# Sinks ahead of the values on 128 rows, and the low parts of x and g last in their groups

## The chip, the cores and the metric

The kernel runs on one core of a Trainium2 chip. The metric is the time of one execution on the device in microseconds; a kernel's time is the median of its runs. The profile comes from one execution, recorded by the hardware profiler. Its engines are PE (matrix products and transposes; PEld is its weight load, which can overlap the product before it), DVE (vector), ACT (scalar functions and copies), POOL and SP (which issues the DMAs).

## The reference

Attention with a window of 128 tokens and 4 sink tokens that every query may see, on q, k, v of shape (4 batches, 8 heads, 768 tokens, 64), then a feed-forward network of 512 to 2048 to 512 on the 3072 rows that come out:

```python
scores = scale * np.matmul(q, k.transpose(0, 1, 3, 2))
keep = is_sink | in_window
scores = np.where(keep, scores, -1000000000.0)
...
a = a / (np.sum(a, axis=-1, keepdims=True) + 1e-09)
x = np.matmul(a, v)            # then (B, S, H*D)
h = x @ w_in
sp = np.maximum(h, 0.0) + np.log1p(np.exp(-np.abs(h)))
g = h * erf(sp)
out = g @ w_out
```

## The kernel before, in words

**Tiling.** The tokens are cut into 12 groups g of 256 (three to a batch), and the 8 heads into 4 pairs c. A pair of heads in a group is one attention step, s = 4g + c, 48 in all. The network works on a group's 512 x 256 slice of x: 16 hidden blocks f of 128 features each, numbered m = 16g + f, of which two share one tile (h_0, h_2, ... h_190 name the pairs).

**An attention step.** `prep` transposes k and q (four products into tqk, L218) and copies them into kq on ACT. `score` makes the scores ps on quarters of the array (sixteen products of 64 x 64, L277); DVE masks them, ACT takes the exponential into pst (L298, four), `norm` divides. `ptrans` transposes the window's part (four products into tp, L322, copied to pt by ACT, L324, and cut to uo by POOL, L328) and the sinks' part (two products into ts, L342, copied to sp by ACT, L346). `av` multiplies with the values (L364) and `avs` with the sinks' values sv (L371), both into one tile av; `xfin` takes it into x.

**Precision.** x, w and g are split into a high and a low part. A hidden block is a sum over four slices c of (high w, high x), (high w, low x) and (low w, high x): twelve products of 128 x 256 on L544, and 24 to a pair. `act` turns a pair into g: on ACT r (L556 to L558) and three u (L561), on DVE three products with acc (L563), of which the first reads h and gives its tile back, then the high part of g on DVE (L568) and the low part on POOL (L569). `project` adds three products (L584 to L586) for each of the group's two output tiles o_0 and o_1. The first group g = 0 is computed in full precision (L540, L581) while the weights are split.

The sinks' part is three rows of 32 for each half i of the group (high, low, high of the 32 probabilities of two heads), 96 rows in all, against sv, whose rows 0 to 31, 32 to 63 and 64 to 95 hold high, high and low of the sinks' values. sv's rows 96 to 127 are zero. At the first group of a batch each step loads its sinks' values anew: POOL clears a corner of the tile v (L198), two DMAs fill it (L200), ACT copies it twice (L226), DVE makes the low part (L227).

**What sets the order.** Each engine works its own list in order. The lists come from a scheduler that simulates the program; each operation carries a priority from the slot a = m + 16 that it belongs to and from its kind (the table O: hidden 0, projections 900, scores and values -300, and so on). `core(s)` issues av of step s - 2, then the scores of s, then avs of s - 2; `follow` ties the first two together in this order. Only among the rest, mainly h and o, does the scheduler choose.

**Tiles that come round.** h has two pairs of banks: h_k and h_(k-4) use the same (pairs are numbered by twos), so h_k's first product waits for the first L563 of h_(k-4). tqk, tp, ts and av go round two banks, so av_s takes the bank of a tp, which is free once ACT has copied pt (L324). tile v has three buffers.

Of the kernel before, what the change touches and what calls it, by code (L numbers as in the profile page):

```python
# [19 lines left out]
P = 128  # L20
# [30 lines left out]
def kernel(  # L51
# [20 lines left out]
    NG = B * GPB  # L72
    NU = 4
    NSTEP = NG * NPAIR
    KB, S3 = P + SW, 6 * SW
    scale = 1.0 / math.sqrt(D)

    cpool = ctx.enter_context(tc.tile_pool(name="const", bufs=1))
# [50 lines left out]
    def fast_path():  # L129
        with ExitStack() as st:  # L130
# [43 lines left out]

            pst = pers.tile([P, RING, 2, 2, KB], F32, name="pst")

            shs = [pers.tile([P, 2, 3, 2 * SW], F32R, name=f"sh{i}") for i in range(2)]
            xp = {}

            stp = {}  # L180
# [48 lines left out]
            def core(s):  # L229

                prev = None
                late = s - AL >= NE
                if late:
                    prev = av(s - AL)
                if s < NSTEP:
                    score(s, prev)
                if late:
                    avs(s - AL)

            def av1(s):  # L240

                av(s)
                avs(s)

            def score(s, prev):

# [67 lines left out]
            def ptrans(s):  # L314
# [15 lines left out]
                        compare_op=op, fill=0.0, base=0, channel_multiplier=sg,  # L330
                    )

                sh = shs[s % 2]
                x = pst[:, s % RING, :, :, P:]
                for r in (0, 2):
                    nc.vector.tensor_copy(sh[:, :, r].rearrange("p i (h t) -> p i h t", h=2), x)
# [2 lines left out]
                    sh[:, :, 0].rearrange("p i (h t) -> p i h t", h=2).bitcast(F32), op=ALU.subtract,  # L339
                )  # L340
                for i in range(2):
                    nc.tensor.transpose(  # L342
                        out=ts[:S3, i, :], in_=sh[:, i].rearrange("p r t -> p (r t)").bitcast(F32), identity=ident
                    )
                sp = d["sp"] = work.tile([P, 2, P], F32R, tag="sp", bufs=AL, name=f"sp_{s}")
                nc.scalar.copy(sp[:S3], ts[:S3])  # L346

            def av(s):

                g, c = divmod(s, NPAIR)  # L350
                gb = g % GPB
                d = stp[s]
                vt = d["v"]
                uo = d["uo"].rearrange("p h i e t -> p h (i e t)")
                a = d["av"] = ps_t.tile([P, GT], F32, tag="t", name=f"av_{s}")
                ops = [(vt[:, 2], uo[:, :, 3 * P :], P), (vt[:, 1], uo[:, :, P : 3 * P], 0)]
                if gb > 0:
                    ops.append((vt[:, 0], uo[:, :, :P], 0))
                prev = None
                for m, (x, y, t0) in enumerate(ops):  # L360
                    for h in range(2):
                        o = a[64 * h : 64 * h + 64, t0 : t0 + y.shape[-1]]
                        prev = follow(
                            prev, nc.tensor.matmul(o, x[:, h, :], y[:, h, :], start=(m == 0), stop=False, skip_group_check=True)  # L364
                        )
                return prev

            def avs(s):

                g, c = divmod(s, NPAIR)  # L370
                nc.tensor.matmul(  # L371
                    stp[s]["av"], sv[:S3, c, :], stp[s]["sp"][:S3].rearrange("p i t -> p (i t)"),
                    start=False, stop=True, skip_group_check=True,
                )

            def xfin(s):

# [18 lines left out]
            def pos(s):  # L396

                return 3 * s if s < NE else 4 * s - 4 * NE + 3 * NE - 2

            plan = {}  # L400
            for s in range(NSTEP + AL):
                if s < NSTEP:
                    for what, fn, a in (
                        ("prep", prep, pos(s) - 3), ("norm", norm, pos(s) + 1), ("ptrans", ptrans, pos(s) + 2),
                        ("load", load, pos(s) - 4),
                    ):
                        plan.setdefault(max(a, 0 if what == "prep" else -1), []).append((what, fn, s))
                plan.setdefault(pos(s), []).append(("core", core, s))
                if s < NE:
                    plan.setdefault(pos(s) + 3, []).append(("av", av1, s))  # L410
                    plan.setdefault(pos(s) + 4, []).append(("xfin", xfin, s))
                elif s - AL >= NE:
                    plan.setdefault(pos(s) + 1, []).append(("xfin", xfin, s - AL))
# [113 lines left out]
    class make_mlp:  # L527
# [7 lines left out]
        def hidden(self, hp, xt, f):  # L535
            j, fs = f // 4, slice(f % 4 * P, f % 4 * P + P)
            o = hp[:, f % 2, :]
            if len(xt) == 1:
                for c in range(NC):
                    nc.tensor.matmul(o, wf[NC * j + c][:, fs], xt[0][:, c, :], start=(c == 0), stop=(c == NC - 1))  # L540
                return
            ops = [(c, *e) for c in range(NC) for e in ((0, 0), (0, 1), (1, 0))]
            for m, (c, p, e) in enumerate(ops):
                nc.tensor.matmul(  # L544
                    o, wt[NC * j + c][:, p, fs], xt[e][:, c, :], start=(m == 0), stop=(m == len(ops) - 1)
# [26 lines left out]
        def project(self, gt, g, f):  # L572
            if f == 0:
                for i in range(2):
                    self.acc[g, i] = self.ps_o.tile([P, DM], F32, tag="o", name=f"o_{g}_{i}")
            for i in range(2):
                o = self.acc[g, i]
                n0 = (f % 2) * GT + i * P
                ws = slice(n0, n0 + P)
                if len(gt) == 1:  # L580
                    nc.tensor.matmul(o, gt[0][:, ws], wf[16 + f], start=(f == 0), stop=(f == NF - 1))  # L581
                    continue
                gh, gl = gt
                nc.tensor.matmul(o, gh[:, ws], wt[16 + f][:, 0, :], start=(f == 0), stop=False)  # L584
                nc.tensor.matmul(o, gh[:, ws], wt[16 + f][:, 1, :], start=False, stop=False)  # L585
                nc.tensor.matmul(o, gl[:, ws], wt[16 + f][:, 0, :], start=False, stop=(f == NF - 1))  # L586

        def result(self, g, i):
            ot = self.work.tile([P, DM], F32, tag="u", bufs=UB, name=f"ot_{g}_{i}")
# [149 lines left out]
```

## Time and profile before

| | before |
|---|---|
| median of three runs | 780.71 us (778.91, 783.86, 780.71) |
| profiled execution: span | 779.7 us |
| PE busy | 728.2 us, 93% of the span |
| ACT busy | 531.3 us, 68% |
| DVE busy | 508.6 us, 65% |
| POOL busy | 204.6 us, 26% |
| from 100 us to the end: PE busy | 661.86 of 679.70 us |

The page gives the profiled execution's span and no separate time for it; the median of the runs is 1.0 us above that span. Busy time counts an engine's instructions and leaves out its waits. A row of a timeline gives the start, the length, the engine and the line, and in brackets how long the engine had been idle before and what released it. Starts on PE are more telling than lengths: products overlap, so the distance between two starts is what a product costs.

### The profile page before, as it was taken

The numbers are of one execution on the slowest core, as the hardware profiler recorded it, in microseconds if no ns is written. First come the engines' busy times: TensorE is split into PE (matmuls) and PEld (weight loads), VectorE is DVE, ScalarE is ACT, GpSimd is POOL, SyncE is SP. The second block draws the span as 40 slices with busy tenths as digits, with TensorE's granted clock in tenths as the row PEclk, the third lists the DMA queues.
The fourth block names the chain that finished last, engine by engine and source line by source line (L and its number), as shares of the span: only waits on it lengthen the run. The fifth ranks groups of instructions, "written<-read, shape, count | busy, mean of one in ns | idle before, by whom it ended". The sixth has DMA issues, their size and how long they took to land.

```text
span 779.7 us, 14925 instructions
## 1 busy us (share of the span) xinstructions
PE 728.2 (93%) x5168; PEld 605.0 (78%) x5168; DVE 508.6 (65%) x1509; ACT 531.3 (68%) x1261; POOL 204.6 (26%) x210
## 2 busy tenths in 40 slices
PE   2578998999999999999999999999999999999997
PEld 1356665788878888888888888888878888888896
DVE  6968999787465576576566476476466476475352
ACT  2245478897687577578688578488578578487474
POOL 1311121133222223232232232232222232232121
PEclk8569899999999999999999999999999999999999
DMA  6765631201211221111121121121121121010000
GB/s 196 241 196 177 228 82 29 70 22 27 70 33 28 59 51 25 48 48 27 32 72 28 41 70 25 34 63 25 31 74 28 28 75 32 11 40 1 27 2 32
DMA packets 100595, 47.33 MB, mean 61 GB/s; under 512 B 89248, under 2 KB 93344, under 8 KB 100512
## 3 DMA queue, kind: packets, MB, share of 16 engines
q1 hardware_dynamic: 100224, 46.29, 21.6%
q8 instruction: 43, 0.70, 0.4%
q14 instruction: 40, 0.33, 0.1%
q10 hardware_dynamic: 288, 0.00, 0.0%
HBM read 37.88 MB, written 6.29 MB: 57 GB/s over the span
## 4 chain that ended last, share of the span: by engine, by line
PE 79%; DVE 9%; ACT 6%; DMA 2%; issue 1%; SPq 1%; POOL 1%; ACTq 0%; DVEq 0%; POOLq 0%
PE h L544 29%; PE o L586 10%; PE o L584 10%; PE o L585 10%; PE av L364 5%; PE ps L277 5%; PE tqk L218 2%; PE tp L322 2%; PE h L540 2%; PE av L371 2%; DVE wt L473 1%; DVE gf L563 1%; ACT pst L298 1%; PE ts L342 1%; DVE w L453 1%
## 5 line engine op out<-in xcount | busy, mean ns | idle before, releaser
L544 PE MATMUL h<-xh,wt 128*128 128x256 f32 x1408 | 271.2, 283 | 5.3 <-DVE acc L563 4.1
L544 PEld LDWEIGHTS h<-xh,wt 128*128 128x128 f32 x1408 | 223.7, 189 | 11.3 <-DVE acc L563 5.6
L544 PE MATMUL h<-xl,wt 128*128 128x256 f32 x704 | 198.7, 283 | 0.0
L569 POOL TENSOR_TENSOR g<-acc,g 128x512 fp32r<-128x512 f32 x88 | 114.9, 1306 | 308.2 <-DVE g L568 211.8
L561 ACT ACTIVATE u<-r 128x512 f32<-128x512 f32 x288 | 163.5, 624 | 10.3 <-DVE wf L459 4.3
L328 POOL TENSOR_SCALAR_AFFINE_SELECT uo<-pt 128x512 f32<-128x512 f32 (+1 forms) x96 | 85.2, 909 | 250.1 <-ACT pt L324 250.1
L584 PE MATMUL o<-wt,g 128*128 128x512 f32 x352 | 141.4, 402 | 0.7 <-DVE g L568 0.7
L585 PE MATMUL o<-wt,g 128*128 128x512 f32 x352 | 139.7, 397 | 0.0
L563 DVE SCALAR_TENSOR_TENSOR acc<-u,h 128x512 f32<-128x512 f32 x88 | 60.4, 687 | 120.8 <-ACT u L561 61.2
L563 DVE SCALAR_TENSOR_TENSOR acc<-u,acc 128x512 f32<-128x512 f32 x176 | 124.7, 709 | 19.9 <-ACT u L561 6.2
L586 PE MATMUL o<-wt,g 128*128 128x512 f32 x352 | 135.3, 401 | 0.3 <-POOL g L569 0.2
L544 PEld LDWEIGHTS h<-xl,wt 128*128 128x128 f32 x704 | 132.9, 189 | 2.3
L298 ACT ACTIVATE pst<-pst,neg 128x144 f32<-128x144 f32 x192 | 77.6, 407 | 39.1 <-DVE neg L294 39.0
L556 ACT ACTIVATE r<-h 128x512 f32<-128x512 f32 x96 | 57.0, 594 | 44.0 <-PE h L544 42.6
L584 PEld LDWEIGHTS o<-wt,g 128*128 128x128 f32 x352 | 66.2, 188 | 13.4 <-ACT r L557 0.9
L586 PEld LDWEIGHTS o<-wt,g 128*128 128x128 f32 x352 | 64.8, 188 | 14.8 <-POOL g L569 1.2
L585 PEld LDWEIGHTS o<-wt,g 128*128 128x128 f32 x352 | 66.1, 188 | 12.1
L289 DVE COPY_PREDICATED ps<-tri,ps 64x256 f32<-64x256 int8 (+1 forms) x100 | 41.8, 420 | 40.3 <-PE ps L277 37.6
L558 ACT ACTIVATE r<-r 128x512 f32<-128x512 f32 x96 | 60.8, 634 | 2.5
L557 ACT ACTIVATE r<-r 128x512 f32<-128x512 f32 x96 | 60.7, 632 | 1.8
L364 PE MATMUL av<-uo,v 128*64 128x128 f32 (+1 forms) x512 | 50.1, 328 | 8.6 <-ACT pt L324 4.4
L388 ACT CAST xh<-av 128x256 fp32r<-128x256 f32 x44 | 16.2, 369 | 59.7 <-PE av L371 59.6
(81 smaller groups left out, 887.5 us busy)
## 6 DMA issues: line engine op xcount, KB each, us to landing
ws<-in_moe_w_in_dram SPq DMA_DIRECT2D x16, 512.0 KB, 5.6
ws<-in_moe_w_out_dram SPq DMA_DIRECT2D x16, 512.0 KB, 5.6
q<-in_q_dram SPq DMA_DIRECT2D x96, 64.0 KB, 2.3
k<-in_k_dram SPq DMA_DIRECT2D x96, 64.0 KB, 2.4
v<-in_v_dram SPq DMA_DIRECT2D x64, 96.0 KB, 2.3
out_dram<-ot SPq DMA_DIRECT2D x24, 256.0 KB, 2.4
v<-in_v_dram SPq DMA_DIRECT2D x32, 64.0 KB, 2.2
kq<-kq SPq DMA_DIRECT2D x32, 64.0 KB, 2.0
```

The lines of the kernel that those rows point to most:

```text
L298: nc.scalar.activation(y, y, AF.Exp, bias=d["neg"][:, i, h : h + 1], scale=-1.0, accum_out=d["sum"][:, i, h : h + 1])
L328: nc.gpsimd.affine_select(out=uo[:, :, i1:, e, :], in_=pt[:, :, i1:, :], pattern=[[0, 2], [0, 2 - i1], [-sg, P]], compare_op=op, fill=0.0, ...
L364: prev, nc.tensor.matmul(o, x[:, h, :], y[:, h, :], start=(m == 0), stop=False, skip_group_check=True)
L544: nc.tensor.matmul(o, wt[NC * j + c][:, p, fs], xt[e][:, c, :], start=(m == 0), stop=(m == len(ops) - 1))
L557: nc.scalar.activation(r, r, AF.Square, bias=b_v, scale=-0.5)
L558: nc.scalar.activation(r, r, AF.Square, bias=b_r)
L561: nc.scalar.activation(u, r, AF.Square, bias=b_a[i], scale=CS)
L563: nc.vector.scalar_tensor_tensor(out=acc, in0=u, scalar=CC[i] * CS**2, in1=x, op0=ALU.add, op1=ALU.mult)
L569: nc.gpsimd.tensor_tensor(gl, acc, gh.bitcast(F32), op=ALU.subtract)
L584: nc.tensor.matmul(o, gh[:, ws], wt[16 + f][:, 0, :], start=(f == 0), stop=False)
L585: nc.tensor.matmul(o, gh[:, ws], wt[16 + f][:, 1, :], start=False, stop=False)
L586: nc.tensor.matmul(o, gl[:, ws], wt[16 + f][:, 0, :], start=False, stop=(f == NF - 1))
```

## The change

Three things are changed. **Sinks.** The tile sh gets a seventh row of 32 that is cleared once on POOL (two tiles, two clearings); the two transposes take 128 rows of it instead of 96, and sp and the sinks' product go over 128 rows. The product stands at the head of `av`, before the values, and opens the sum over the whole tile; `avs` is gone, and the scores are the last part of `core`. **Hidden.** The twelve products of a block are put as the eight with the high part of x (high and low w for each c) and then the four with its low part. **Projection.** The three products of both output tiles alternate: (high g, high w) for o_0 and o_1, then (high g, low w), then (low g, high w). The number of products, transposes and copies stays the same.

```diff
--- before.py
+++ after.py
@@ -72,7 +72,7 @@
     NG = B * GPB
     NU = 4
     NSTEP = NG * NPAIR
-    KB, S3 = P + SW, 6 * SW
+    KB = P + SW
     scale = 1.0 / math.sqrt(D)
 
     cpool = ctx.enter_context(tc.tile_pool(name="const", bufs=1))
@@ -174,7 +174,9 @@
 
             pst = pers.tile([P, RING, 2, 2, KB], F32, name="pst")
 
-            shs = [pers.tile([P, 2, 3, 2 * SW], F32R, name=f"sh{i}") for i in range(2)]
+            shs = [pers.tile([P, 7, 2 * SW], F32R, name=f"sh{i}") for i in range(2)]
+            for x in shs:
+                nc.gpsimd.memset(x[:, 6].bitcast(F32), 0.0)
             xp = {}
 
             stp = {}
@@ -229,18 +231,10 @@
             def core(s):
 
                 prev = None
-                late = s - AL >= NE
-                if late:
+                if s - AL >= NE:
                     prev = av(s - AL)
                 if s < NSTEP:
                     score(s, prev)
-                if late:
-                    avs(s - AL)
-
-            def av1(s):
-
-                av(s)
-                avs(s)
 
             def score(s, prev):
 
@@ -330,7 +324,7 @@
                         compare_op=op, fill=0.0, base=0, channel_multiplier=sg,
                     )
 
-                sh = shs[s % 2]
+                sh = shs[s % 2][:, :6].rearrange("p (i r) t -> p i r t", i=2)
                 x = pst[:, s % RING, :, :, P:]
                 for r in (0, 2):
                     nc.vector.tensor_copy(sh[:, :, r].rearrange("p i (h t) -> p i h t", h=2), x)
@@ -339,11 +333,10 @@
                     sh[:, :, 0].rearrange("p i (h t) -> p i h t", h=2).bitcast(F32), op=ALU.subtract,
                 )
                 for i in range(2):
-                    nc.tensor.transpose(
-                        out=ts[:S3, i, :], in_=sh[:, i].rearrange("p r t -> p (r t)").bitcast(F32), identity=ident
-                    )
+                    x = shs[s % 2][:, 3 * i : 3 * i + 4].rearrange("p r t -> p (r t)").bitcast(F32)
+                    nc.tensor.transpose(out=ts[:, i, :], in_=x, identity=ident)
                 sp = d["sp"] = work.tile([P, 2, P], F32R, tag="sp", bufs=AL, name=f"sp_{s}")
-                nc.scalar.copy(sp[:S3], ts[:S3])
+                nc.scalar.copy(sp, ts)
 
             def av(s):
 
@@ -356,22 +349,17 @@
                 ops = [(vt[:, 2], uo[:, :, 3 * P :], P), (vt[:, 1], uo[:, :, P : 3 * P], 0)]
                 if gb > 0:
                     ops.append((vt[:, 0], uo[:, :, :P], 0))
-                prev = None
+                prev = nc.tensor.matmul(
+                    a, sv[:, c, :], d["sp"].rearrange("p i t -> p (i t)"),
+                    start=True, stop=False, skip_group_check=True,
+                )
                 for m, (x, y, t0) in enumerate(ops):
                     for h in range(2):
                         o = a[64 * h : 64 * h + 64, t0 : t0 + y.shape[-1]]
                         prev = follow(
-                            prev, nc.tensor.matmul(o, x[:, h, :], y[:, h, :], start=(m == 0), stop=False, skip_group_check=True)
+                            prev, nc.tensor.matmul(o, x[:, h, :], y[:, h, :], start=False, stop=(m == len(ops) - 1), skip_group_check=True)
                         )
                 return prev
-
-            def avs(s):
-
-                g, c = divmod(s, NPAIR)
-                nc.tensor.matmul(
-                    stp[s]["av"], sv[:S3, c, :], stp[s]["sp"][:S3].rearrange("p i t -> p (i t)"),
-                    start=False, stop=True, skip_group_check=True,
-                )
 
             def xfin(s):
 
@@ -407,7 +395,7 @@
                         plan.setdefault(max(a, 0 if what == "prep" else -1), []).append((what, fn, s))
                 plan.setdefault(pos(s), []).append(("core", core, s))
                 if s < NE:
-                    plan.setdefault(pos(s) + 3, []).append(("av", av1, s))
+                    plan.setdefault(pos(s) + 3, []).append(("av", av, s))
                     plan.setdefault(pos(s) + 4, []).append(("xfin", xfin, s))
                 elif s - AL >= NE:
                     plan.setdefault(pos(s) + 1, []).append(("xfin", xfin, s - AL))
@@ -539,7 +527,7 @@
                 for c in range(NC):
                     nc.tensor.matmul(o, wf[NC * j + c][:, fs], xt[0][:, c, :], start=(c == 0), stop=(c == NC - 1))
                 return
-            ops = [(c, *e) for c in range(NC) for e in ((0, 0), (0, 1), (1, 0))]
+            ops = [(c, p, 0) for c in range(NC) for p in range(2)] + [(c, 0, 1) for c in range(NC)]
             for m, (c, p, e) in enumerate(ops):
                 nc.tensor.matmul(
                     o, wt[NC * j + c][:, p, fs], xt[e][:, c, :], start=(m == 0), stop=(m == len(ops) - 1)
@@ -573,17 +561,15 @@
             if f == 0:
                 for i in range(2):
                     self.acc[g, i] = self.ps_o.tile([P, DM], F32, tag="o", name=f"o_{g}_{i}")
-            for i in range(2):
-                o = self.acc[g, i]
-                n0 = (f % 2) * GT + i * P
-                ws = slice(n0, n0 + P)
-                if len(gt) == 1:
-                    nc.tensor.matmul(o, gt[0][:, ws], wf[16 + f], start=(f == 0), stop=(f == NF - 1))
-                    continue
-                gh, gl = gt
-                nc.tensor.matmul(o, gh[:, ws], wt[16 + f][:, 0, :], start=(f == 0), stop=False)
-                nc.tensor.matmul(o, gh[:, ws], wt[16 + f][:, 1, :], start=False, stop=False)
-                nc.tensor.matmul(o, gl[:, ws], wt[16 + f][:, 0, :], start=False, stop=(f == NF - 1))
+            ops = ((0, 0), (0, 1), (1, 0)) if len(gt) > 1 else ((0, 0),)
+            for m, (e, p) in enumerate(ops):
+                w = wt[16 + f][:, p, :] if len(gt) > 1 else wf[16 + f]
+                for i in range(2):
+                    n0 = (f % 2) * GT + i * P
+                    nc.tensor.matmul(
+                        self.acc[g, i], gt[e][:, n0 : n0 + P], w,
+                        start=(f == 0 and m == 0), stop=(f == NF - 1 and m == len(ops) - 1),
+                    )
 
         def result(self, g, i):
             ot = self.work.tile([P, DM], F32, tag="u", bufs=UB, name=f"ot_{g}_{i}")
```

**Order on PE, first place:** the first step of group 6, from the sinks' transposes of step 25 (ts_25) to the values of 24 (av_24), its sinks' product, and the scores of 26. x2 stands for two equal instructions in a row. Before:

```order
L342 MATMUL ts_25_4313<-ident_61,sh1_143 96x128 x2
L364 MATMUL av_24_4396<-uo_24_4146,v_24_3874 64x128 x2
L364 MATMUL av_24_4396<-uo_24_4146,v_24_3874 64x256 x2
L277 MATMUL ps_26_4403<-kq_137 64x208 x2
L277 MATMUL ps_26_4403<-kq_137 64x224 x2
L277 MATMUL ps_26_4403<-kq_137 64x208 x2
L277 MATMUL ps_26_4403<-kq_137 64x224 x2
L371 MATMUL av_24_4396<-sp_24_4154,sv_139 128x256
L544 MATMUL h_84_4503<-xh_5_3707,wt_4_1092 128x256
L544 MATMUL h_84_4503<-xl_5_3708,wt_4_1092 128x256
...
L218 MATMUL tqk_27_4464<-ident_61,k_27_4427 128x128 x2
```

And now:

```order
L337 MATMUL ts_25_4315<-ident_61,sh1_143 128x128 x2
L532 MATMUL h_84_4505<-xh_5_3709,wt_4_1094 128x256 x2
L532 MATMUL h_84_4505<-xh_5_3709,wt_5_1151 128x256 x2
...
L532 MATMUL h_84_4505<-xl_5_3710,wt_7_1234 128x256
L352 MATMUL av_24_4398<-sp_24_4156,sv_139 128x256
L360 MATMUL av_24_4398<-uo_24_4148,v_24_3876 64x128 x2
L360 MATMUL av_24_4398<-uo_24_4148,v_24_3876 64x256 x2
L271 MATMUL ps_26_4406<-kq_137 64x208 x2
L271 MATMUL ps_26_4406<-kq_137 64x224 x2
L271 MATMUL ps_26_4406<-kq_137 64x208 x2
L271 MATMUL ps_26_4406<-kq_137 64x224 x2
L220 MATMUL tqk_27_4466<-ident_61,k_27_4429 128x128 x2
```

The sinks' product (sp_24, sv) has gone from behind ps_26 to ahead of the values of av_24, ps_26 is followed by the transposes of tqk_27 at once, and between ts_25 and av_24 stands h_84 as a whole.

**Order on ACT, second place:** the first group of a batch (s = 12 to 15), around the copies of the sinks' values of step 15 (sv from v_15). r_35 and u0_35 belong to the pair h_34, r_37 to h_36. Before:

```order
L556 ACTIVATE r_35_2292<-h_34_2189 128x512
...
L557 ACTIVATE r_35_2292<-r_35_2292 128x512
L226 CAST sv_139<-v_15_2236 32x128 x2
L558 ACTIVATE r_35_2292<-r_35_2292 128x512
L298 ACTIVATE pst_141,sum_14_2207<-pst_141,neg_14_2208 128x144 x2
L221 COPY kq_137<-tqk_15_2270 128x4x128
...
L298 ACTIVATE pst_141,sum_14_2207<-pst_141,neg_14_2208 128x144
L561 ACTIVATE u0_35_2297<-r_35_2292 128x512
...
L556 ACTIVATE r_37_2366<-h_36_2309 128x512
```

And now:

```order
L544 ACTIVATE r_35_2294<-h_34_2191 128x512
...
L545 ACTIVATE r_35_2294<-r_35_2294 128x512
L546 ACTIVATE r_35_2294<-r_35_2294 128x512
L549 ACTIVATE u0_35_2299<-r_35_2294 128x512
...
L544 ACTIVATE r_37_2368<-h_36_2311 128x512
...
L545 ACTIVATE r_37_2368<-r_37_2368 128x512
L228 CAST sv_139<-v_15_2238 32x128 x2
L546 ACTIVATE r_37_2368<-r_37_2368 128x512
L292 ACTIVATE pst_141,sum_14_2210<-pst_141,neg_14_2211 128x144 x2
L549 ACTIVATE u0_37_2373<-r_37_2368 128x512
```

The copies from v_15 stood inside the chain of r_35, ahead of u0_35; now that chain is done before them, and they stand inside the chain of r_37.

**Order on PE, third place:** between the pairs h_34 and h_36, at the same batch boundary. Before:

```order
L322 MATMUL tp_13_2118<-ident_61,pst_141 128x128
L544 MATMUL h_34_2189<-xl_2_1503,wt_3_1060 128x256
L544 MATMUL h_34_2189<-xh_2_1502,wt_3_1060 128x256
L342 MATMUL ts_13_2119<-ident_61,sh1_143 96x128 x2
L364 MATMUL av_12_2202<-uo_12_1952,v_12_1680 64x128 x2
L364 MATMUL av_12_2202<-uo_12_1952,v_12_1680 64x256 x2
L277 MATMUL ps_14_2209<-kq_137 64x208 x2
L277 MATMUL ps_14_2209<-kq_137 64x224 x2
...
L371 MATMUL av_12_2202<-sp_12_1960,sv_139 128x256
L544 MATMUL h_36_2309<-xh_2_1502,wt_4_1092 128x256
```

And now:

```order
L532 MATMUL h_34_2191<-xl_2_1505,wt_3_1062 128x256
L569 MATMUL o_1_0_1582<-wt_31_1631,g_31_2116 128x512
L569 MATMUL o_1_1_1583<-wt_31_1631,g_31_2116 128x512
...
L316 MATMUL tp_13_2120<-ident_61,pst_141 128x128
L569 MATMUL o_1_1_1583<-wt_31_1631,g_31_2116 128x512
L316 MATMUL tp_13_2120<-ident_61,pst_141 128x128 x2
L337 MATMUL ts_13_2121<-ident_61,sh1_143 128x128 x2
L532 MATMUL h_36_2311<-xh_2_1504,wt_4_1094 128x256 x2
L532 MATMUL h_36_2311<-xh_2_1504,wt_5_1151 128x256 x2
...
L352 MATMUL av_12_2204<-sp_12_1962,sv_139 128x256
L360 MATMUL av_12_2204<-uo_12_1954,v_12_1682 64x128 x2
```

Projections of group 1 now stand ahead of the transposes, and h_36 follows ts_13 directly, where av_12, the scores ps_14 and the sinks' product stood before it.

## Rows read from the trace of the kernel before

**Rows 1.** The page's first part: busy us of each engine (share of the span), instructions.
```profile
PE 728.2 (93%) x5168; PEld 605.0 (78%) x5168; DVE 508.6 (65%) x1509; ACT 531.3 (68%) x1261; POOL 204.6 (26%) x210
```
**Rows 2.** Windows: from:to, length, busy (instructions) of PE, PEld, DVE, ACT, POOL, clock, DMA.
```profile
100.00:779.70 679.70, 661.86 (x4796) 559.55 (x4795) 428.61 (x1249) 488.33 (x1140) 186.88 (x182) 1.00 0.16 40
...
218.00:222.00 4.00, 4.00 (x21) 3.92 (x20) 2.57 (x9) 3.06 (x6) 1.28 (x1) 0.57 0.00 0
```
**Rows 3.** Waits of PE: waiting line, what it waits for, total us, times, longest.
```profile
PE av L364 <- ACT pt L324: 4.4, 10, 0.5
...
PE h L544 <- DVE acc L563: 4.1, 4, 1.8
```
**Rows 4.** Timeline of PE, 400 to 417 us: start, length, line, names, shapes.
```profile
402.94 0.39 PE L371 MATMUL av<-sp,sv 96*128 96x256 f32 x1
403.17 0.38 PE L218 MATMUL tqk<-ident,k 128*128 128x128 f32 x2
...
404.18 0.39 PE L544 MATMUL h<-xh,wt 128*128 128x256 f32 x2
...
404.52 0.39 PE L544 MATMUL h<-xh,wt 128*128 128x256 f32 x2
...
409.06 0.39 PE L584 MATMUL o<-wt,g 128*128 128x512 f32 x1
409.29 0.39 PE L585 MATMUL o<-wt,g 128*128 128x512 f32 x1
...
415.42 0.40 PE L544 MATMUL h<-xh,wt 128*128 128x256 f32 x2
...
415.77 0.40 PE L544 MATMUL h<-xh,wt 128*128 128x256 f32 x2
```
**Rows 5.** Groups by line and form, weight loads: busy, mean ns | idle before, releasers.
```profile
L218 PEld LDWEIGHTS tqk<-ident,k 128*128 128x128 f32 x96 | 12.3, 148 | 7.4 <-issue 7.2
...
L371 PEld LDWEIGHTS av<-sp,sv 96*128 96x128 f32 x48 | 9.1, 190 | 16.6 <-issue 16.2 <-ACT pst L298 0.4
```
**Rows 6.** Timeline of all engines around 562 us.
```profile
561.82 0.58 ACT L324 COPY pt<-tp 128x512 f32<-128x512 f32 x1
...
562.46 0.87 PE L364 MATMUL av<-uo,v 128*64 128x128 f32 x8 [0.46 <-ACT pt L324]
```
**Rows 7.** Timeline of PE, 155.9 to 156.6 us.
```profile
156.23 0.39 PE L544 MATMUL h<-xh,wt 128*128 128x256 f32 x1 [0.27 <-DVE acc L563]
```
**Rows 8.** Timeline of all engines, 563 to 573 us, a batch's first group.
```profile
563.44 0.20 POOL L198 MEMSET v<- 32x128 f32 x1
...
567.86 0.62 ACT L226 CAST sv<-v 32x128 fp32r<-32x128 f32 x2 [1.38 <-DMA v<-in_v_dram]
...
570.80 0.62 ACT L561 ACTIVATE u<-r 128x512 f32<-128x512 f32 x1
...
571.53 0.69 DVE L563 SCALAR_TENSOR_TENSOR acc<-u,h 128x512 f32<-128x512 f32 x1 [3.05 <-ACT u L561]
...
572.27 0.39 PE L544 MATMUL h<-xh,wt 128*128 128x256 f32 x1 [1.69 <-DVE acc L563]
```
**Rows 9.** Timeline of all engines, 197 to 208 us, step 13 at a batch's first group.
```profile
197.40 0.99 PE L277 MATMUL ps<-kq 64*64 64x208 f32 x16
...
200.90 0.62 ACT L226 CAST sv<-v 32x128 fp32r<-32x128 f32 x2 [1.03 <-DMA v<-in_v_dram]
...
202.76 0.40 ACT L298 ACTIVATE pst<-pst,neg 128x144 f32<-128x144 f32 x1
...
204.28 0.60 ACT L556 ACTIVATE r<-h 128x512 f32<-128x512 f32 x1 [1.03 <-PE h L544]
...
206.11 0.57 ACT L324 COPY pt<-tp 128x512 f32<-128x512 f32 x1
...
206.58 1.15 ACT L561 ACTIVATE u<-r 128x512 f32<-128x512 f32 x2
...
207.24 0.69 DVE L563 SCALAR_TENSOR_TENSOR acc<-u,h 128x512 f32<-128x512 f32 x1 [2.14 <-ACT u L561]
```

## The prediction, made before the changed kernel ran

> **What bounds the kernel now.** I read the page's head first [rows 1]: PE is busy for 728.2 of 779.7 us, the next engine (ACT) for 531.3. Then the windows [rows 2]: from 100 us to the end PE is busy for 661.86 of 679.70 us, so 18 us of idle time are all that a better order can win there, unless products themselves get cheaper. The other 728.2 − 661.9 = 66 us of PE's work lie in the first 100 us, where PE waits for weights and for DVE; the order changes little there, and I carry ±2.5 us for it. Next, the waits of PE [rows 3]. Most of the list is from the start-up; two lines recur in the steady part: values waiting for the copy pt on ACT (4.4 us, ten times, never over 0.5) and hidden products waiting for DVE's first acc (4.1 us, four times, up to 1.8). Last, the timeline of PE for the price of one product [rows 4]: three h products take 404.52 − 404.18 = 0.34 us in one stretch (113 ns each) and 415.77 − 415.42 = 0.35 in another (118 ns); an o product takes 409.29 − 409.06 = 0.23 us. So PE sets the pace, and the change is worth the waits that it takes from PE or gives it.
>
> **The change, part by part.**
>
> *The sinks' product on 128 rows.* Products, transposes and copies keep their count. Rows stream in parallel, so 128 rows for 96 cost PE nothing in columns streamed: 256 before and after. The transposes' weight load grows by 32 columns; the load of 128 columns is 148 ns [rows 5], beside other products, and I cost it at nothing (bounds 0 and 96 × 0.037 = 3.6 us, were the added quarter of it exposed 96 times; it hides behind the product before it, as h's do). The two clearings on POOL, 0.2 us each by the nearest row [rows 8], stand among the program's first instructions, long before the first step's sinks; 0.4 would be their bound.
>
> *Its new place.* Behind the scores the sinks' product costs 403.17 − 402.94 = 0.23 us [rows 4], twice an h product of the same size, because the first full-array product behind the 64 x 64 ones exposes weight load: 0.23 − 0.118 = 0.11. After the change a transpose of tqk stands there in 38 of 42 steps by the order. Its load is 148 ns for 190 [rows 5], so I take 0.11 − 0.042 = 0.07 exposed, a gain of 0.042 × 38 = **−1.6 us**. The bounds are 0 (a transpose pays as much) and −4.6 (0.11 × 42, nothing exposed). The number of changes between whole-array and quarter-array products per step stays as it was, since the sinks' product now stands before the values.
>
> On the price of such a load the Trainium skill ("TensorE: Matmul & The Clock Gate", section "LDWEIGHTS (loading the stationary operand)") says that it goes by the columns loaded alone, columns / 1.2 in ns, 107 for both of these. By that this term would be 0 and the sum 1.6 us less of a gain; [rows 5] speak against it, 148 and 190 ns for the same 128 columns.
>
> *Values waiting for pt.* In nine steps of the steady part, the first of each group from 12 to 44, the sinks' transposes are followed directly by the values of the step before, and av needs the bank that tp held, until ACT has copied it: pt starts at 561.82 and takes 0.58, and PE stands for 0.46 until 562.46 [rows 6]. In the new order (first place) the 24 products of a hidden pair, 24 × 0.118 = 2.8 us, stand between; pt is done long before. The tenth wait, of 0.5, lies in the start-up, so these nine are 4.4 − 0.5 = 3.9 us [rows 3]: **−3.9 us**. What covers pt is this pair; the bounds are −4.4 and 0, the latter if h cannot start there itself.
>
> *Hidden products waiting for acc.* Three of the four [rows 3] follow a batch's first group; the fourth is that of 0.27 us at 156.23, in the start-up [rows 7]. At 563.44 the corner of v is cleared, and only at 567.86, 4.4 us later, do the sinks' values reach ACT, which stood idle for 1.38 us for them [rows 8]; ACT works in order, and behind them stand the exponentials and the u of the pair before (u0_35 at the first of these boundaries, the second place of the change). So u starts at 570.80, acc at 571.53, and PE stands until 572.27, for 1.69 us: its next pair needs the bank that acc reads. In the new order u0_35 stands ahead of these copies. They then hold up r_37's chain. Let T0 be the start of ps_14: the sinks' values come 4.4 us after their clearing and the exponentials follow, which puts the release by acc at about T0 + 8.1, while PE, with the 24 h products that now stand elsewhere and its projections, needs it at about T0 + 10.1 (estimates from the order and the prices above). So three waits go: 4.1 − 0.27 = **−3.9 us**. Bounds: −3.9, and 0 if r_37's chain comes 2 us later than that and waits in the same way.
>
> Behind the longest of these waits, of 1.8 us, the granted clock was 0.57 from 218 to 222 us [rows 2], with 21 products in 4 us: 4.0 − 21 × 0.13 (a mean of h, o and transposes there) = 1.2. **−1.2 us** if the wait goes, 0 if not.
>
> *New risk: the cover of a group's third pair.* h_(16g+4) needs the bank of h_(16g). Between the two, PE had 4.4 to 4.8 us of other work by the order; now 4.2 (18 h products, 6 o, tp and ts), and at g = 3, 6, 9 only 3.2 (2 o). What must fit is ACT's r to u and DVE's first acc: in the trace 206.58 − 204.28 = 2.30 from r to u with a pt copy between, 0.66 to acc's start, 0.69 for it [rows 9], so 3.65 with that copy and about 3.6 with the lag before r and less of the copy. So 4.2 covers it and 3.2 misses by 0.3, three times. At the batch boundaries (h_36, h_84, h_132) the exponentials stand ahead of r: from ps at 197.40 on, the copies sv end at 201.52 and the last exponential at 203.16 [rows 9]; if r follows at once, with 1.9 to u where no pt stands between, acc ends 9.0 to 9.2 us behind ps, and by the order PE asks for the bank at 9.2: on the edge, 0.2 three times. Together **+1.5 us**; bounds 0 and +6.
>
> *Hidden and projection orders.* The low part of x is read four products later, the low part of g two. Both are ready in the steady part by the waits of PE (for the low g only 0.2 us in all, left in the early part), so 0 there; the first steps now need sp before the values, **+0.3**.
>
> Sum: −1.6 − 3.9 − 3.9 − 1.2 + 1.5 + 0.3 = −8.8 us. The profiled span is 779.7, the median of the runs 1.0 above; I keep that 1.0: 780.7 − 8.8, about **772 us**.
>
> **The rivals.**
>
> *B, the gain is eaten (chance 0.28, 776 to 782 us).* The waits of [rows 3] go, but PE meets others: ACT is 68% busy [rows 1] and its list is shuffled, so a copy or u comes late where PE now asks earlier. The same time results if the order helps only the av waits and the boundary waits move to r_37's chain: 780.7 − 3.9 = 776.8. For it: each wait is short, and the slack found is under 1 us in places. Against: by the order the cover shrinks at the third pairs only.
>
> *C, products get cheaper (0.14, 764 to 768).* h products run at 113 ns in some stretches and 118 in most [rows 4]. There are 11 × 16 × 12 = 2112 of them; 5 ns on most of these is some 8 us, and as the sequence of products is new, more of them may come at 113 (or those that do now may come at 118, for 1 to 2 us the other way). What decides between the two the trace does not show.
>
> *D, slower (0.10, 784 to 793).* The place is the third pair of each group. The chain of 3.6 us against a cover of 4.2 must hold eleven times. If ACT is late by 2.0 to 2.5 us (four exponentials of 0.4 and their reads stand ahead of r, as from 201.52 to 203.16 in [rows 9], and the copies sp and pt), each group loses 1.4 to 1.9: 15 to 21 us, against the 8.8 won: 787 to 793; some groups spared, 784. It decides from a lateness of 0.6 us on (4.2 − 3.6), and at 1.4 the gain is used up (0.8 × 11 = 8.8).
>
> *The forecast (0.42, 768.5 to 775).* Both families of waits gone, little new. The remaining 0.06 lie outside all of these.
>
> **How the numbers follow.** A measurement of this kernel can tell about 1%, 7.8 us, from no change: faster means under 772.9, slower over 788.5. The forecast lies below 772.9 with 0.28 of its 0.42; with C and a little of the rest, faster is 0.44. B, the rest of the forecast and the low half of D are within 1%: 0.48. Slower is the high half of D and a little of the rest, 0.08. The likeliest case gives 772. The range takes in the forecast, B, C and the low edge of D, which also covers the start-up's ±2.5 and the bounds of the load and of the third pairs: 764 to 785, with some 0.15 left out.
>
> **What would show it.** Right: in the waits of PE the line of av (now the sinks' product) on pt is gone from the steady part, and so is that of h on acc at the batch boundaries; the product behind ps is a transpose, about 0.05 us sooner; no stretch of granted clock near 0.57 after 200 us. Wrong: a line of h on acc with about eleven entries (D), a line of the sinks' product on sp, or of o on the low g; long idle times of ACT for the sinks' values; or the waits gone and the busy time of PE, rather than its idle time, changed by several us (C, or its reverse).

## The result, and the profile after

The changed kernel takes 772.9 us (median of six runs, 772.2 to 774.8) against 780.8 (778.9 to 783.9): a ratio of 0.989, with a 95% interval of 0.986 to 0.992. The forecast was 772. The profiled execution's span is 770.8 us against 779.7. Here an execution's time lies about 2.0 us above its span (772.8 and 770.8), so the profiled execution of before, with a span of 779.7, is by this estimate some 1 us slower than the median one. This would be why the two profiles differ by 8.9 us and the medians by 7.9.

The page's first part of the changed kernel, to compare with [rows 1]:

```profile
PE 726.0 (94%) x5168; PEld 602.1 (78%) x5168; DVE 524.6 (68%) x1509; ACT 536.4 (70%) x1261; POOL 204.4 (27%) x212
```

With as many instructions PE is busy for 2.2 us less; the other 6.7 us that went are idle time. The waits of PE (total, times, longest) between 250 and 700 us show it, first before:

```profile
PE av L364 <- ACT pt L324: 3.6, 8, 0.5
PE h L544 <- DVE acc L563: 2.1, 2, 1.7
```

and after:

```profile
PE h L532 <- DVE acc L551: 0.8, 3, 0.3
PE tp L316 <- DVE pst L306: 0.3, 1, 0.3
```

The waits on pt are gone from this stretch, and so are the two on acc behind a batch boundary; three of 0.3 on acc, at other places, are new. At the first batch boundary the windows answer to [rows 2]:

```profile
214.00:218.00 4.00, 4.00 (x25) 3.44 (x24) 3.60 (x7) 3.90 (x11) 0.91 (x1) 1.00 0.03 6
218.00:222.00 4.00, 4.00 (x34) 3.79 (x33) 3.76 (x10) 3.46 (x7) 1.85 (x3) 1.00 0.00 0
```

PE is busy throughout, and 34 products, not 21, fit into 218 to 222 us at full clock. Why is in the timelines of ACT and PE there, after the change ([rows 8] show the same work at the third boundary of the kernel before):

```profile
206.59 1.15 ACT L549 ACTIVATE u<-r 128x512 f32<-128x512 f32 x2
...
211.44 0.62 ACT L228 CAST sv<-v 32x128 fp32r<-32x128 f32 x2 [1.17 <-DMA v<-in_v_dram]
...
213.42 1.14 ACT L549 ACTIVATE u<-r 128x512 f32<-128x512 f32 x2
```

```profile
211.17 0.64 PE L532 MATMUL h<-xh,wt 128*128 128x256 f32 x4
```

ACT still stands 1.17 us for the sinks' values. But the u of the pair that PE needs next (h_34, released for h_38 at 211.17) now starts at 206.59, ahead of them, and the u behind them, at 213.42, belongs to a pair that PE does not ask for so soon. The row of PE has no bracket: it waited for nothing.

Behind the scores (382.51, sixteen products) stands a transpose now, as in [rows 4] the sinks' product:

```profile
382.51 0.99 PE L271 MATMUL ps<-kq 64*64 64x208 f32 x16
383.42 0.44 PE L220 MATMUL tqk<-ident,k 128*128 128x128 f32 x2
383.70 0.38 PE L220 MATMUL tqk<-ident,q 128*128 128x128 f32 x2
```

The two transposes of k take 383.70 − 383.42 = 0.28 us where two in the stream take 0.22: about 0.055 us is exposed, half of the sinks' product's 0.11. The sinks' product itself costs nearly as much in its new place (0.21 us to the start of the values, 0.23 behind the scores); but the h product ahead of the values, which took 0.21 before, now takes 0.12 ahead of it. Over a whole step, from the product ahead of the attention's to the one behind tqk, PE needs 0.05 us less, and that in every step of the steady part with the same kinds of work next to it.

### The profile page after: what moved, and what is told of

Its sections match the earlier page's. It is cut to its first block, busy times and chain, and to the rows that moved or that the text cites. A ratio compares the mean times of both kernels' runs of the same rounds, so it can differ in the third digit from the quotient of the medians.

```text
span 770.8 us, 14942 instructions
## 1 busy us (share of the span) xinstructions
PE 726.0 (94%) x5168; PEld 602.1 (78%) x5168; DVE 524.6 (68%) x1509; ACT 536.4 (70%) x1261; POOL 204.4 (27%) x212
## 4 chain that ended last, share of the span: by engine, by line
PE 74%; DVE 13%; ACT 5%; DMA 4%; issue 2%; POOL 1%; SPq 1%; ACTq 0%; DVEq 0%; POOLq 0%
PE o L569 29%; PE h L532 28%; PE av L360 5%; PE ps L271 4%; PE tqk L220 3%; PE tp L316 2%; DVE acc L551 2%; DVE w L441 2%; DVE pst L306 2%; ACT pst L292 1%; DVE w L438 1%; PE ts L337 1%; DMA out_dram<-ot 1%; DVE gf L551 1%; POOL g L557 1%
## 5 line engine op out<-in xcount | busy, mean ns | idle before, releaser
L569 PE MATMUL o<-wt,g 128*128 128x512 f32 x1056 | 273.6, 401 | 1.3 <-POOL g L557 0.5
L532 PE MATMUL h<-xh,wt 128*128 128x256 f32 x1408 | 206.4, 283 | 1.5 <-DVE acc L551 0.8
L532 PEld LDWEIGHTS h<-xh,wt 128*128 128x128 f32 x1408 | 186.7, 188 | 11.7 <-DVE acc L551 1.6
L532 PE MATMUL h<-xl,wt 128*128 128x256 f32 x704 | 113.0, 280 | 0.0
L532 PEld LDWEIGHTS h<-xl,wt 128*128 128x128 f32 x704 | 95.7, 188 | 0.0
L306 DVE TENSOR_SCALAR pst<-pst,sum 128x144 f32<-128x144 f32 x192 | 58.0, 364 | 1.5
L556 DVE CAST g<-acc 128x512 fp32r<-128x512 f32 x88 | 44.2, 502 | 15.2 <-PE o L569 11.4
L316 PE MATMUL tp<-ident,pst 128*128 128x128 f32 x192 | 36.3, 289 | 17.5 <-DVE pst L306 17.1
L223 ACT COPY kq<-tqk 128x512 f32<-128x512 f32 x48 | 28.1, 586 | 33.8 <-PE tqk L220 33.8
L271 PE MATMUL ps<-kq 64*64 64x208 f32 (+1 forms) x768 | 49.6, 370 | 0.1
```

Of the source, the lines that this page charges most:

```text
L271: nc.tensor.matmul(ps[h][hf, x : x + n], qt[r, hf], kt[r, r0 : r0 + n], start=True, stop=True),
L306: nc.vector.tensor_scalar_mul(p, p, sm[:, i, h : h + 1])
L532: nc.tensor.matmul(o, wt[NC * j + c][:, p, fs], xt[e][:, c, :], start=(m == 0), stop=(m == len(ops) - 1))
L569: nc.tensor.matmul(self.acc[g, i], gt[e][:, n0 : n0 + P], w, start=(f == 0 and m == 0), stop=(f == NF - 1 and m == len(ops) - 1),)
```

## Where the time went, by segments

One execution is not enough for this: each kernel was profiled twice (e10 and e11 below are the second times). The table gives the time that each needs for a stretch, less what the first profile of before needs for it. Stretches are bounded by the first products of hidden pairs. Six o products that stood ahead of h_34 stand behind it in the changed order, and one more stands ahead of h_176; they are added or taken off at 0.2335 us each. The first boundary and the steady part stand in one row, because at their border (h_40) a whole attention step changes sides, and its price is known to some 0.5 us only.

| stretch | before, 2nd | after | after, 2nd | predicted |
|---|---|---|---|---|
| start to h_34 | −1.2 | −3.2 | −2.4 | +0.3 |
| h_34 to h_176: first boundary and steady part | +0.7 | −8.1 | −9.4 | −9.1 |
| h_176 to the last product | 0.0 | +1.7 | +0.5 | 0 |
| behind it | +0.4 | +0.6 | +0.6 | 0 |
| span | −0.1 | −8.9 | −10.6 | −8.8 |

The last column sorts the terms of the forecast by where they lie. The second row holds nearly all of them, and on the mean of each kernel's two profiles it came as priced. On the same means the start gave some 2.5 us more than expected, and the end took some 1.5 of it back.

## The experiments

All times are medians; ratios are to the kernel before on the same chip.

**e1, the sinks' part alone.** Of the change only its first part; hidden products and projections as before:

```diff
-            ops = [(c, p, 0) for c in range(NC) for p in range(2)] + [(c, 0, 1) for c in range(NC)]
+            ops = [(c, *e) for c in range(NC) for e in ((0, 0), (0, 1), (1, 0))]
...
```

> The first part of the change alone (sinks' product on 128 rows at the head of av; hidden products and projections as before). My theory: the gain is an order of work on PE that takes away two families of waits and one exposed weight load per step, and this part alone moves h_36, h_84 and h_132 ahead of av_12, av_24 and av_36. By its order the values follow the sinks' transposes directly only at steps 16, 28 and 40, so waits on pt stay there (3 x 0.4) and go at the other six (-2.7); the boundary waits go (-3.9, and -1.2 of clock); the place behind the scores gives -1.7; third pairs h_36, h_84, h_132 have a cover of 3.7 for a chain of 3.6 and more, up to +1. Sum: 771 to 774 us. Rival A (the hidden order makes the gain): 778 to 781. Rival B (128 rows cost weight load): 780 or more.

773.2 us, 0.990 (0.987 to 0.992): the whole gain. The waits of PE from 190 to 700 us:

```profile
PE av L352 <- ACT pt L318: 1.5, 3, 0.5
PE tp L316 <- DVE pst L306: 0.6, 1, 0.6
```

Three waits on pt, at steps 16, 28 and 40, where the order still has the values right behind the sinks' transposes; none at the six steps where other work stands between; none on acc. This shows within one kernel what takes these waits away. Both rivals of this expectation fall.

**e2, the hidden order alone.**

```diff
-            ops = [(c, *e) for c in range(NC) for e in ((0, 0), (0, 1), (1, 0))]
+            ops = [(c, p, 0) for c in range(NC) for p in range(2)] + [(c, 0, 1) for c in range(NC)]
```

> The order of the hidden products alone. By its order one to eight hidden products come between the sinks' transposes and the values at the first step of each group, so waits on pt shrink to 0 to 0.3 each (-2.5); av still comes ahead of the next pair at the batch boundaries, where the cover of h_38 is 8.5 us as before, so the boundary waits stay; the sinks' product stays behind the scores. My theory: 777 to 779 us, with the three long waits of h on acc still in the list. Rival A (the hidden order makes the gain): 771 to 774.

780.4 us, 0.998 (0.996 to 0.999): a miss. From 190 to 700 us its waits are

```profile
PE tp L322 <- DVE pst L312: 1.1, 2, 0.7
PE h L544 <- DVE acc L563: 0.8, 3, 0.3
PE o L586 <- POOL g L569: 0.4, 2, 0.2
```

so the waits on pt went here too, and the long ones on acc in part, though u0_35 still stands behind the sinks' values on ACT. At the first boundary ACT now stands 0.57 us for those values (1.45 before), the transposes of the window's part stand ahead of the next pair and wait 0.73 for the normalized probabilities, and 0.27 is left on acc: 1.0 in place of 1.76. From h_34 to h_176 this order so wins 5.0 us. But up to h_34 it loses 4.7 against before (waits of o on ACT's pst, 1.2, and of h on acc, 1.0, among them; for its clock see the last section), and the two nearly cancel.

**e3, the order of the projections alone.**

```diff
-            for i in range(2):
-                o = self.acc[g, i]
...
+            for m, (e, p) in enumerate(ops):
+                for i in range(2):
...
```

> The order of the projections alone; the rest of PE's order is that of before. My theory: no wait of the two families changes. The last block's two output tiles end 0.23 us apart and not 0.7, so the tail behind the last product grows by 0.5 to 0.7, and at the change of groups the two products of the first block need both banks at once: 781 to 782 us. Rival: the low part of g read later takes the early waits of o on g away: 779 to 780.

782.7 us, 1.002 (1.000 to 1.004), 0.7 above the range of my theory. What the theory said of the waits holds: both families stay (3.9 and 3.8 us from 190 to 700 us). Against the first profile of before, the stretch from h_176 to the last product is 0.8 us longer and what lies behind it 0.6.

**e4, the whole change but the projections.**

```diff
-            ops = ((0, 0), (0, 1), (1, 0)) if len(gt) > 1 else ((0, 0),)
-            for m, (e, p) in enumerate(ops):
+            for i in range(2):
+                o = self.acc[g, i]
...
```

> The whole change without the order of the projections. PE's order is that of the changed kernel but for the sequence within a projection. My theory: all that the changed kernel won stays, and it loses its longer tail (0.66 us) and the waits around 727 to 735 us (some 1 us): 771 to 772.5 us. Rival (alternating the output tiles is part of the gain): 774 to 777.

774.6 us, 0.991 (0.989 to 0.993): outside what I expected, in the range of the rival, and not to be told from the changed kernel's interval. In its profile one product at the last group stands long:

```profile
736.98 0.50 PE L572 MATMUL o<-wt,g 128*128 128x512 f32 x1 [1.44 <-DVE g L556]
```

Another of 0.51 follows, the granted clock is 0.72 from 738 to 744 us, and from h_176 to the last product this profile needs 4.0 us more than before's. It was taken in the slowest of the six runs (777.7). Whether alternating tiles has a gain of its own stays open.

**e5, 96 rows in the new place.**

```diff
-            shs = [pers.tile([P, 7, 2 * SW], F32R, name=f"sh{i}") for i in range(2)]
+            shs = [pers.tile([P, 6, 2 * SW], F32R, name=f"sh{i}") for i in range(2)]
...
-                    nc.tensor.transpose(out=ts[:, i, :], in_=x, identity=ident)
+                    nc.tensor.transpose(out=ts[:S3, i, :], in_=x, identity=ident)
...
```

> The changed kernel with the sinks' product and its transposes on 96 rows instead of 128, in their new place; the order of PE is the same row by row. My theory: the rows cost nothing either way, only the place and the order matter: within 2 us of the changed kernel, 771 to 775 us, and the load of the sinks' transposes 130 ns for 145. Rival B (the whole array in use saves something at the switch from quarter-array products, or the wider load costs): 776 us or more, or under 770.

The edit puts the copy sp and the product itself on 96 rows as well. 774.2 us, 0.991 (0.988 to 0.995), as expected. PE's order is that of the changed kernel row by row, and so is the price of the sinks' product (groups by line and form: busy, mean ns | idle before):

```profile
L335 PEld LDWEIGHTS ts<-ident,sh 128*96 128x96 f32 x96 | 11.5, 129 | 10.8 <-issue 6.6 <-DVE pst L304 0.7 <-PE ps L269 0.3
L350 PE MATMUL av<-sp,sv 96*128 96x256 f32 x48 | 14.7, 306 | 1.4 <-ACT sp L337 1.4
```

With 128 rows its 48 products are busy for the same 14.7 us. The rows are worth nothing that these runs can tell, either way.

**e6, before with the sinks' values on POOL.**

```diff
-                    for r0 in (0, 32):
-                        nc.scalar.copy(sv[r0 : r0 + 32, c, :], d["sv"])
-                    nc.vector.tensor_tensor(sv[64:96, c, :], d["sv"], sv[:32, c, :].bitcast(F32), op=ALU.subtract)
+                    for r0 in (0, 32):
+                        nc.gpsimd.tensor_copy(sv[r0 : r0 + 32, c, :], d["sv"])
+                    nc.gpsimd.tensor_tensor(sv[64:96, c, :], d["sv"], sv[:32, c, :].bitcast(F32), op=ALU.subtract)
```

> The kernel before, with the sinks' values copied and subtracted on POOL instead of ACT and DVE, so that ACT no longer stands for their DMA at a batch's first group; values still directly behind the sinks' transposes (nine times). My theory: the three long waits of h on acc (3.9 us) vanish without any change of place, and the waits of the values on pt (4 us) stay: 776.5 to 779 us. Rival C (u and acc are late there because ACT is full, not because it waits for the DMA): 780 to 782 and the waits stay above 1 us.

775.7 us, 0.992 (0.990 to 0.995). The waits of PE from 190 to 700 us are one line:

```profile
PE av L364 <- ACT pt L324: 4.3, 9, 0.5
```

The waits on acc are gone without any change of place, those on pt stand. What held u back was ACT's wait for the DMA together with the copies behind it. The edit takes both from ACT; by [rows 8] the wait is 1.38 us of them and the copies 0.62, and PE stood for 1.69, so by these rows the copies alone would not have made it. The rival that ACT is simply full falls. The time lies 0.8 us below the range I gave; that expectation left out the low clock behind the first boundary, which is not in this profile either.

**e7, the changed kernel with the sinks' values on POOL** (the same edit).

> The changed kernel with the sinks' values copied and subtracted on POOL. By its order the cover of h_52, h_100 and h_148 goes from 3.2 to 4.2 us. My theory: their three waits (0.3 each) and the waits of tp on the normalized probabilities at the batch boundaries (0.4 each) go: 770 to 772.5 us. Rival: POOL, which now stands for the DMA, delivers the low part of g late, and o waits for it: 774 us or more.

770.6 us, 0.987 (0.983 to 0.990, four runs), as expected. The three waits on acc are gone; of those of tp at the batch boundaries, which were to go as well, one is left, PE's only wait from 190 to 700 us:

```profile
PE tp L316 <- DVE pst L306: 0.4, 1, 0.4
```

**e8, e7 with the first and the last block's projections in the old sequence.**

```diff
+            seq = [(m, i) for m in range(len(ops)) for i in range(2)]
+            if f in (0, NF - 1):
+                seq.sort(key=lambda x: x[1])
...
```

> As the run before it, and in the first and the last block of each group the projections of the two output tiles stand one after the other again (three products each) instead of alternating. My theory: the tail behind the last product shrinks by 0.4 to 0.7, the wait of the first block for its bank (0.6 at the last group) too: 769 to 771.5 us. Rival (the end is set by the network's own chain of the last group): as the run before it.

768.45 us, 0.985 (0.982 to 0.988), just below the range I gave: the shortest time of all, some 12 us below the kernel before. From h_176 to the last product it loses 0.2 us where e7 lost 1.5, and behind that product it takes 0.4 less than e7.

**e9, e1 with the sinks' values on POOL** (the edits of e1 and e6).

> The first part of the change alone, with the sinks' values copied and subtracted on POOL; hidden products and projections in the order of before. By its order the third pairs have a cover of 3.2 to 3.7 us in eight groups and 4.4 to 5.2 in three, and the values follow the sinks' transposes directly at step 16 only. My theory (a cover under 3.5 costs 0.3 each, and the orders of hidden products and projections add nothing of their own): 770 to 772 us. Rival (the new order within hidden products or projections has a gain of its own, which the changed kernel with the same edit had at 770.6): 773 us or more.

773.7 us, 0.990 (0.985 to 0.994): nothing on top of e1, a miss in the range of the rival, though the interval also holds 771. Its profile lost 2.8 us to e1's before h_34; from h_40 to h_176 it needs 3.5 us more than e7, of which its waits in the list (0.7 on acc, 0.5 on pt, against e7's 0.4) give 0.8. The order within hidden products may have a part of its own once nothing else waits; I cannot say how.

**e10 and e11, both kernels once more** (no edit).

> The kernel before once more, for a second profile. My theory: the waits on pt (nine, 0.2 to 0.5) and on acc (three at the batch boundaries, 1.8, 0.4 and 1.7) come again at the same places, and the early waits of the values on uo and of the scores on neg too, since they hang on the order; the low granted clock behind the wait at 216 us need not come again. Rival: the low clock comes with the wait each time.

> The changed kernel once more, for a second profile. My theory: the waits of h_52, h_100 and h_148 on acc (0.3 each) and those of the last group come again; the time from the first hidden product of the second pair to that of the fourth (20.6 us in the profile of the changed kernel, 23.3 in that of before) goes with the granted clock and may differ. Rival: it is 20.6 again, and belongs to the change.

781.6 and 771.0 us. All named waits came again, but for those at 733 to 735 us in the changed kernel's first profile. On the clock my theory was half right. The time from h_4 to h_8 was 22.3 us in both second profiles, after 23.3 and 20.6: it does not belong to the kernel. It goes with the granted clock from 76 to 85 us: 20.6 us in the three profiles where that is 1.00, 22.3 in the five at 0.81, and 23.2 to 23.4 in the five at 0.62 to 0.70. But the low clock behind the boundary wait did come again in e10 (the product, then the window):

```profile
215.37 0.38 PE L544 MATMUL h<-xh,wt 128*128 128x256 f32 x1 [1.76 <-DVE acc L563]
```

```profile
216.00:220.00 4.00, 4.00 (x23) 4.00 (x23) 2.67 (x11) 3.53 (x6) 1.29 (x1) 0.59 0.00 0
```

while in e3, with a wait a little shorter, the clock stayed:

```profile
215.79 0.39 PE L544 MATMUL h<-xh,wt 128*128 128x256 f32 x1 [1.61 <-DVE acc L563]
```

```profile
216.00:220.00 4.00, 4.00 (x32) 3.86 (x32) 2.70 (x11) 3.87 (x8) 1.29 (x1) 1.00 0.00 0
```

## Why the prediction was right

- *Values waiting for pt, −3.9:* right. All nine are gone, and e1 ties them to what stands between.
- *Hidden products waiting for acc, −3.9:* right, and e6 shows the cause by itself. My estimate that the copies would hold up only r_37's chain, without harm, is what the rows at 206.59 and 213.42 show. With T0 = 206.95, acc gives the bank back at 214.83, T0 + 7.9 (estimated 8.1), and PE asks for it at 216.80, T0 + 9.9 (estimated 10.1):

```profile
214.14 0.69 DVE L551 SCALAR_TENSOR_TENSOR acc<-u,h 128x512 f32<-128x512 f32 x1 [1.45 <-ACT u L549]
```

- *The clock, −1.2:* right in kind, a little small (4.0 − 21 × 0.13 is 1.27 to begin with). e3 prices it: with the same products in the same order up to their sequence within a projection, it needs 22.4 us from h_34 to h_40 at full clock where before needs 24.1 in both profiles; its wait is 0.15 shorter, so the low clock costs some 1.5. It came behind that wait in both profiles of before.
- *The new place, −1.6:* right; about 0.055 us is exposed behind the scores for 0.11, and the 0.05 of a whole step comes to 1.9 in 38 steps. By the rule of the Trainium skill on weight loads ("TensorE: Matmul & The Clock Gate", section "LDWEIGHTS (loading the stationary operand)") it would have been 0; the rows at 382.51 to 383.70 speak against that.
- *The third pairs, +1.5:* the three with a cover of 3.2 us wait as forecast, by 0.3:

```profile
261.22 0.72 PE L532 MATMUL h<-xh,wt 128*128 128x256 f32 x4 [0.28 <-DVE acc L551]
```

  The three at the batch boundaries, "on the edge", do not wait at all: 0.8 in place of 1.5. Rival D asked for eleven.
- *128 rows, 0:* right (e5).
- *The start, +0.3:* wrong. On the mean of the profiles the start is some 2 us shorter. Before, the values of step 1 stood for POOL, and the next steps behind them:

```profile
37.70 1.55 PE L364 MATMUL av<-uo,v 128*64 128x128 f32 x8 [2.81 <-POOL uo L328]
```

  After, the product on sp goes first (with the wait of 0.46 that I had priced), and the values find uo ready in this profile:

```profile
36.39 0.39 PE L352 MATMUL av<-sp,sv 128*128 128x256 f32 x1 [0.46 <-ACT sp L339]
36.71 0.87 PE L360 MATMUL av<-uo,v 128*64 128x128 f32 x8
```

  The wait on uo (4.2 us in two, 5.0 in e10, 4.5 in e3) is 0 to 1.9 in the eight profiles with the sinks' part; I saw the added wait and not the one that goes. Not all of it is won: before 190 us the waits of tp on DVE's pst are 16.8 us for 11.4, while that of the scores on neg, 3.0, is gone. Another 1 to 3 us of the start differ from one execution to the next, so 2 us is a rough figure.
- *The end, 0:* wrong by some 1.5. Alternating tiles lets both end together and asks for both banks of the next group at once: e3, which only alternates, loses 0.8 and 0.6 us there, and e8 takes most of it back. e4, without alternating, had a long wait of its own there instead.

Start and end missed in opposite directions, so it is in part luck that the total came so near. The prediction's rival C (cheaper products) did not come: the share of h products at 115 ns or less, from h_40 to h_176, is 14% and 5% in the two profiles of before and 3% in both of after, so it is mostly chance, and went slightly the other way. Rival B's place, r_37's chain, was free.

## What to carry to other kernels

Where one engine paces a kernel, count what stands between the releaser and the waiting product on that engine: the change won by two covers (24 products ahead of the values, one chain ahead of a DMA wait), and the prices of these two could be read from the trace of before. An in-order engine that waits for a DMA passes its wait on to everything queued behind it; moving that copy to an idle engine (e6) gave as much as reordering did for that term. And profile the same kernel twice before a difference of 2 us in one stretch is explained.

## What was not expected of the hardware

The granted clock fell behind a wait of 1.76 us of PE in both profiles of before (0.57 and 0.59 over 4 us) and not behind one of 1.61 us at the same place in e3. The length of the wait alone does not decide it: in e4 the clock fell (0.72 from 738 to 744 us) behind waits of 1.44 and 0.51.

In the start-up the clock differs between executions of one kernel, and moved the stretch from h_4 to h_8 between 20.6 and 23.4 us over the profiles. Another low stretch there goes with the order of the hidden products. From 120 to 137 us the granted clock is 0.80 to 0.90 in all seven profiles with the new order of hidden products, and 1.00 in all six with the old one. First before, then after:

```profile
120.00:137.00 17.00, 14.03 (x77) 8.28 (x76) 15.89 (x39) 14.47 (x33) 1.86 (x2) 1.00 0.09 20
120.00:137.00 17.00, 14.19 (x69) 7.55 (x67) 15.26 (x40) 13.56 (x33) 1.85 (x2) 0.90 0.09 20
```

Ahead of it a transpose of tp waits 1.26 to 1.27 us in those seven, where the six others have 0.91 to 0.95. What this costs was not tried, and the prediction has no term for it; it may be part of what e2 lost before h_34.
